# Splitting the state-read matmuls of an f32 attention-and-MLP kernel over two 64-column tiles of the TensorE array

## The chip, the cores and the metric

One core of a Trainium2 chip runs the whole program. The metric is the device time of one execution in microseconds (us); the profiled span is some 2 us shorter than the time of the same run. "Granted clock" is the share of the full TensorE clock that the trace records, 1.0 or 0.5. Kernels of one session are compared with runs of the kernel before on the same chip. "Batch" means one of the eight batch elements of the attention, which the kernel interleaves with the MLP of the batch before it.

## The reference, cut to what matters

```python
B, H, S, Ns, D = 8, 8, 512, 32, 64
scores2 = scale * state @ x^T                      # [B, H, Ns, S]
a2 = exp(scores2 - max); a2 /= a2.sum(-1)          # softmax over the 512 tokens
sread = a2 @ x                                     # [B, H, Ns, D]: the reads of the states
...                                                # xread, the other direction, likewise
h = concat(xread, sread) @ w_in                    # 4352 rows, 512 -> 2048
out = (h * cos(h)) @ w_out                         # 2048 -> 512
```

Everything is f32. The change concerns `sread` alone: for each head a product of 32 x 512 by 512 x 64.

## The kernel before

The eight heads are four pairs (index k) of two (index j). `a2T[:, j, c]` holds the weights of chunk c of 128 tokens, transposed: 128 tokens x (4 pairs x 32 states). One matmul multiplies all 128 columns with the x of all four pairs (256 columns), and of its four by four blocks only the diagonal ones are wanted: pair k's states with pair k's x. `keep` picks them, and `keep2` transposes what it picked for the MLP.

```python
def reads(self, j):
    cols = slice(NK * D * j, NK * D * j + NK * D)      # NK = 4, D = 64: 256 columns
    for c in range(NC):                                # 4 chunks of 128 tokens
        nc.tensor.matmul(
            out=at[:, 0, cols], lhsT=self.a2T[:, j, c, :],
            rhs=self.x_b[:, c].rearrange("p (k j) d -> p j k d", j=2)[:, j],
            start=(c == 0), stop=(c == NC - 1))

def keep(self):
    self.inverse(self.i2)
    src = at[:, 0].rearrange("p (j k d) -> p j k d", j=2, k=NK)
    for k in range(NK):
        rows = slice(Ns * k, Ns * k + Ns)
        nc.vector.tensor_tensor(self.sr[rows], src[rows, :, k, :], ..., op=ALU.mult)
...
LATE = ([("turn", j) for j in range(2)] + [("reads", j) for j in range(2)]
        + [("keep",), ("keep2",)])
```

Around it runs the MLP: `hidden` (two matmuls of 512 columns), the gate on ScalarE and VectorE, `output` (four matmuls of 512 columns). The attention's parts of the next batch are dealt out between them, so one call of `reads` stands before an `output` block and the other before a `hidden` block. `products` and `scores` already use array tiles (64 rows x 32 columns, eight at once). In the first 165 us VectorE and ScalarE also convert the weights, which come as float64.

## Time and profile before

| | before |
|---|---|
| time, median of 3 | 903.25 us (902.56 to 905.52) |
| profiled span | 901.1 us, granted clock 0.973 |
| PE busy | 841.5 us, 93% |
| reads on PE (L311) | 128 instructions, 32.0 us |
| one batch in the saturated part | 94.87 us, PE busy all of it |

From about 170 us on PE works almost without a pause. Before that PE waits for the converted weights and its clock comes and goes, as the page's clock row shows (40 slices of the span, tenths of full speed):

```profile
PEclk9689988999999999999999999999999999999999
```

### The profile page before, as it was taken

Reading aid. Unit: us, or ns where it says so; the run is one execution under the profiler, and the core shown is the slowest. Engines: PE = TensorE matmul, PEld = TensorE weight load, DVE = VectorE, ACT = ScalarE, POOL = GpSimd, SP = SyncE. Lnnn points to the kernel's source line nnn. Section 1 sums busy time; section 2 is a strip of 40 time slices with the busy share of each in tenths; the row PEclk is TensorE's granted clock in tenths of the full one; section 3 lists DMA queues with packets and bytes.
Section 4 is the critical chain, followed back from the end, with each engine's and each line's share of the span. In section 5 each row is a group of like instructions: output and inputs, shape, how many; then the busy total and the mean of one; then the engine's idle time right before and its main releaser. Section 6 shows DMA issues by size and latency. Waiting matters only on the chain.

```text
span 901.1 us, 7084 instructions
## 1 busy us (share of the span) xinstructions
PE 841.5 (93%) x2720; PEld 385.2 (43%) x2720; DVE 356.7 (40%) x520; ACT 408.9 (45%) x631; POOL 0.7 (0%) x6
## 2 busy tenths in 40 slices
PE   3569867899999999999999999999999999999997
PEld 2134324244534453444444443445344534444664
DVE  4687885335322443245224522353225322222121
ACT  2546563355344634464344525453455344434332
POOL 0000000000000000000000000000000000000000
PEclk9689988999999999999999999999999999999999
DMA  6632630021000300030003000300010000000100
GB/s 163 186 141 96 184 140 1 0 70 24 1 1 23 71 0 1 1 93 1 0 1 93 1 0 1 91 4 1 1 47 1 0 1 23 24 0 1 47 1 23
DMA packets 45377, 35.05 MB, mean 39 GB/s; under 512 B 36384, under 2 KB 36384, under 8 KB 45344
## 3 DMA queue, kind: packets, MB, share of 16 engines
q1 hardware_dynamic: 44256, 34.35, 13.4%
q8 instruction: 21, 0.34, 0.2%
q10 hardware_dynamic: 1088, 0.26, 0.2%
q14 instruction: 12, 0.10, 0.0%
HBM read 25.69 MB, written 8.91 MB: 38 GB/s over the span
## 4 chain that ended last, share of the span: by engine, by line
PE 86%; DVE 7%; ACT 4%; issue 1%; DMA 0%; ACTq 0%; DVEq 0%
PE o L403 48%; PE h L373 28%; PE at L245 5%; PE at L311 3%; PE at L219 1%; DVE e L176 1%; ACT e L165 1%; ACT raw L166 1%; DVE w_in L189 1%; PE at L300 1%; DVE w_in L179 1%; ACT q L379 1%; ACT q L388 1%; DVE w_out L189 1%; DVE q L382 1%
## 5 line engine op out<-in xcount | busy, mean ns | idle before, releaser
L403 PE MATMUL o<-w_out,g 128*128 128x512 f32 x1088 | 495.3, 597 | 5.9 <-DVE w_out L189 5.9
L403 PEld LDWEIGHTS o<-w_out,g 128*128 128x128 f32 x1088 | 204.4, 192 | 249.3 <-issue 236.7
L373 PE MATMUL h<-aT,sw 128*128 128x512 f32 x512 | 250.9, 613 | 4.1 <-ACT sw L343 3.4
L382 DVE SCALAR_TENSOR_TENSOR q<-q,h 128x512 f32<-128x512 f32 (+1 forms) x144 | 94.3, 655 | 348.0 <-ACT q L379 348.0
L379 ACT ACTIVATE q<-h 128x512 f32<-128x512 f32 (+1 forms) x144 | 82.5, 573 | 276.1 <-PE h L373 276.1
L393 DVE TENSOR_TENSOR g<-h,q 128x512 f32<-128x512 f32 (+1 forms) x144 | 95.2, 661 | 158.9 <-ACT q L388 158.7
L373 PEld LDWEIGHTS h<-aT,sw 128*128 128x128 f32 x512 | 96.4, 195 | 128.3 <-issue 111.2
L387 ACT ACTIVATE q<-q 128x512 f32<-128x512 f32 (+1 forms) x144 | 87.2, 606 | 105.2 <-DVE q L382 105.2
L388 ACT ACTIVATE q<-q,halfpi 128x512 f32<-128x512 f32 (+1 forms) x144 | 100.5, 698 | 4.5
L245 PE MATMUL at<-w_in,stT 64*32 64x512 f32 (+1 forms) x528 | 41.6, 606 | 24.1 <-DVE w_in L189 12.2
L343 ACT COPY sw<-at 128x1024 f32<-128x1024 f32 (+1 forms) x33 | 32.3, 978 | 43.6 <-PE at L245 43.6
L311 PE MATMUL at<-x_b,a2T 128*128 128x256 f32 x128 | 32.0, 396 | 4.0 <-DVE a2T L303 4.0
L311 PEld LDWEIGHTS at<-x_b,a2T 128*128 128x128 f32 x128 | 25.3, 199 | 13.9 <-issue 6.5
L373 PE MATMUL h<-sT,w_in 128*128 128x256 f32 x128 | 30.2, 379 | 0.0
L245 PEld LDWEIGHTS at<-w_in,stT 64*32 64x32 f32 x528 | 6.8, 106 | 54.8 <-DVE w_in L189 17.8
L373 PEld LDWEIGHTS h<-sT,w_in 128*128 128x128 f32 x128 | 24.3, 190 | 10.1 <-issue 5.0
L409 ACT ACTIVATE ot<-o 128x512 f32<-128x512 f32 x34 | 19.4, 596 | 19.8 <-DMA out_dram<-ot 14.7
L165 ACT ACTIVATE e<-e,ebias 128x1024 int32<-128x1024 int32 (+1 forms) x18 | 18.9, 1051 | 11.4 <-DVE e L162 11.4
L219 PEld LDWEIGHTS at<-ident,x_b 128*128 128x128 f32 x112 | 13.8, 141 | 16.7 <-issue 12.0
L263 DVE STREAM_TRANSPOSE spread<-m 128x1024 f32<-128x1024 f32 x16 | 19.8, 1236 | 0.0
L176 DVE SCALAR_TENSOR_TENSOR e<-raw,e 128x1024 int32<-128x1024 int32 (+1 forms) x18 | 19.7, 1096 | 0.0
L226 ACT COPY xT<-at 128x512 f32<-128x512 f32 x28 | 16.0, 571 | 8.1 <-PE at L219 8.1
(49 smaller groups left out, 269.5 us busy)
## 6 DMA issues: line engine op xcount, KB each, us to landing
x_b<-in_x_dram SPq DMA_DIRECT2D x32, 256.0 KB, 4.7
raw<-in_moe_w_out_dram SPq DMA_DIRECT2D x8, 1024.0 KB, 4.8
out_dram<-ot SPq DMA_DIRECT2D x32, 256.0 KB, 2.2
raw<-in_moe_w_in_dram SPq DMA_DIRECT2D x6, 1024.0 KB, 5.2
raw<-in_moe_w_in_dram SPq DMA_DIRECT2D x4, 512.0 KB, 5.4
out_dram<-ot SPq DMA_DIRECT2D x8, 64.0 KB, 1.7
st<-in_state_dram ACTq DMA_DIRECT2D x4, 64.0 KB, 3.2
st<-in_state_dram SPq DMA_DIRECT2D x4, 64.0 KB, 3.0
```

The source lines that it names most:

```text
L165: nc.scalar.activation(e, e, func=ACTF.Relu, bias=ebias, scale=8.0)
L176: nc.vector.scalar_tensor_tensor(out=e, in0=raw[:, :, :, 1], scalar=-2 ** 31, in1=e, op0=ALU.bitwise_and, op1=ALU.bitwise_or)
L245: nc.tensor.matmul(out=at[Ns * k:Ns * k + Ns, j, 0:n], lhsT=w[D * j:D * j + D, self.b, Ns * k:Ns * k + Ns], rhs=r(slice(D * j, D * j + D), k),
L311: nc.tensor.matmul(out=at[:, 0, cols], lhsT=self.a2T[:, j, c, :], rhs=self.x_b[:, c].rearrange("p (k j) d -> p j k d", j=2)[:, j], start=( ...
L343: nc.scalar.copy(sw_of[self.b, nt][:, :, c0:c1], at[:, :, 0:c1 - c0])
L373: nc.tensor.matmul(out=t.hp, lhsT=t.lhs(i), rhs=t.rhs(i), start=(i == 0), stop=(i == t.kn - 1))
L379: nc.scalar.activation(t.q, t.hp, func=ACTF.Copy, bias=MAGIC)
L382: nc.vector.scalar_tensor_tensor(out=t.q, in0=t.q, scalar=MAGIC, in1=t.hp, op0=ALU.subtract, op1=ALU.subtract)
L387: nc.scalar.activation(t.q, t.q, func=ACTF.Abs)
L388: nc.scalar.activation(t.q, t.q, func=ACTF.Sin, bias=halfpi, scale=-TWO_PI)
L393: nc.vector.tensor_tensor(t.g[:, 0:t.n], t.hp, t.q, op=ALU.mult)
L403: nc.tensor.matmul(out=acc[i], lhsT=t.g[:, P * i:P * i + P], rhs=w_out[:, t.f, :], start=(t.f == 0), stop=(t.f == NF - 1))
```

## The change

Intent: of the sixteen blocks that `reads` computes, twelve are thrown away. Two tiles of 64 array columns take two pairs each, and each streams only the 128 columns of its own pairs, so that eight of the sixteen are no longer computed; both tiles are to run at the same time. A switch between whole-array instructions and tiles is called a mode change below. Its price in the trace has two parts: the drain, a gap of some 93 ns before the next block starts, and the exposed load, the first weight load of that block, which no streaming hides.

```diff
         def reads(self, j):
-            cols = slice(NK * D * j, NK * D * j + NK * D)
+            cols = slice(2 * D * j, 2 * D * j + 2 * D)
             for c in range(NC):
-                nc.tensor.matmul(
-                    out=at[:, 0, cols], lhsT=self.a2T[:, j, c, :],
-                    rhs=self.x_b[:, c].rearrange(...)[:, j],
-                    start=(c == 0), stop=(c == NC - 1))
+                x_c = self.x_b[:, c].rearrange("p (k j) d -> p j k d", j=2)
+                for k in range(0, NK, 2):
+                    rows = slice(Ns * k, Ns * k + 2 * Ns)
+                    nc.tensor.matmul(
+                        out=at[rows, 0, cols], lhsT=self.a2T[:, j, c, rows],
+                        rhs=x_c[:, j, k:k + 2], start=(c == 0),
+                        stop=(c == NC - 1), tile_position=(0, Ns * k))

         def keep(self):
-            src = at[:, 0].rearrange("p (j k d) -> p j k d", j=2, k=NK)
+            src = at[:, 0, 0:4 * D].rearrange("p (j k d) -> p j k d", j=2, k=2)
...
-                    self.sr[rows], src[rows, :, k, :],
+                    self.sr[rows], src[rows, :, k % 2, :],
```

More of the change, by code (lines that the diff above doesn't have):

```diff
@@ L308, in reads @@
         def reads(self, j):
-            cols = slice(NK * D * j, NK * D * j + NK * D)
+            cols = slice(2 * D * j, 2 * D * j + 2 * D)
             for c in range(NC):
-                nc.tensor.matmul(
-                    out=at[:, 0, cols], lhsT=self.a2T[:, j, c, :],
-                    rhs=self.x_b[:, c].rearrange("p (k j) d -> p j k d",
-                                                 j=2)[:, j],
-                    start=(c == 0), stop=(c == NC - 1))
+                x_c = self.x_b[:, c].rearrange("p (k j) d -> p j k d", j=2)
[5 more added lines that the diff above has]
+                        stop=(c == NC - 1), tile_position=(0, Ns * k))
         def keep(self):
             self.inverse(self.i2)
-            src = at[:, 0].rearrange("p (j k d) -> p j k d", j=2, k=NK)
+            src = at[:, 0, 0:4 * D].rearrange("p (j k d) -> p j k d", j=2,
+                                              k=2)
             for k in range(NK):
```

## The prediction

> **What bounds the kernel now.** I read the page first, then the stretch table over single batches, then PE's waits, then PE's timeline inside one batch, then the chain of waits.
>
> The page's busy row and its rows for the changed instruction (engine, operation, operands, count | busy us, mean ns | idle before):
>
> ```profile
> PE 841.5 (93%) x2720; PEld 385.2 (43%) x2720; DVE 356.7 (40%) x520; ACT 408.9 (45%) x631; POOL 0.7 (0%) x6
> ...
> L311 PE MATMUL at<-x_b,a2T 128*128 128x256 f32 x128 | 32.0, 396 | 4.0 <-DVE a2T L303 4.0
> L311 PEld LDWEIGHTS at<-x_b,a2T 128*128 128x128 f32 x128 | 25.3, 199 | 13.9 <-issue 6.5
> ```
>
> To see: 8 batches x 2 head halves x 4 chunks are 64 matmuls of the source, but x128 records: each f32 matmul is two load-and-multiply pairs. All reads together are 32.0 us of PE, so even a reads that cost nothing could save 3.5% at most.
>
> The stretch table (stretch, length, busy time of each engine, granted clock, DMA):
>
> ```profile
> 235.26:330.13 94.87, 94.87 (x314) 42.33 (x313) 33.25 (x49) 44.03 (x68) 0.00 (x0) 1.00 0.09 23
> 330.13:425.00 94.87, 94.87 (x314) 42.33 (x313) 33.25 (x49) 44.03 (x68) 0.00 (x0) 1.00 0.09 23
> ...
> 0.00:160.00 160.00, 109.46 (x351) 49.33 (x352) 114.12 (x149) 79.56 (x107) 0.70 (x6) 0.86 0.43 128
> ```
>
> To see: from about 235 us on PE is busy the whole of every 94.87 us batch at full clock, VectorE for 33 us and ScalarE for 44 us of it. PE's waits after 240 us, asked for alone, are an empty list. A microsecond taken from PE there is a microsecond of the end. Before 160 us it is different: PE 109 of 160 us, VectorE 114 (the weights' conversion), clock 0.86.
>
> PE's timeline in the third batch (start, length, PE, line, operation, count):
>
> ```profile
> 236.99 3.60 PE L403 MATMUL o<-w_out,g 128*128 128x512 f32 x8
> 240.42 1.89 PE L311 MATMUL at<-x_b,a2T 128*128 128x256 f32 x8
> 242.15 1.88 PE L373 MATMUL h<-aT,sw 128*128 128x512 f32 x4
> ...
> 252.75 1.88 PE L373 MATMUL h<-aT,sw 128*128 128x512 f32 x4
> 254.56 1.09 PE L245 MATMUL at<-w_in,stT 64*32 64x512 f32 x16
> 255.58 3.70 PE L403 MATMUL o<-w_out,g 128*128 128x512 f32 x8
> 259.21 1.09 PE L245 MATMUL at<-w_in,stT 64*32 64x512 f32 x16
> ```
>
> To see: one call of reads runs from 240.42 to 242.15: 1.73 us, 216 ns an instruction, pure streaming. L403 takes (240.42-236.99)/8 = 429 ns for twice the columns, so nothing but columns counts. And L245, the products, already run as array tiles (64 rows x 32 columns, eight of them): 16 instructions that would take 16 x 427 ns = 6.8 us one after the other take 1.02 us. This block is my measuring stick.
>
> **What the Trainium skill says.** (1) "TensorE: Matmul & The Clock Gate", Part 3: Packing small matmuls, says that matmuls on different column tiles of the array run at the same time, three of 32 columns measured at 2.38x. The trace agrees for the products: records of single instructions put the eight first starts at 254.558 to 254.605 us, 7 ns apart, and the eight second ones at 255.012 to 255.058. These overlap across column tiles on the same rows too, which the reads need. (2) The same section says that a weight load overlaps a running matmul only when the row group differs. The products disagree: the second load of a tile starts at 254.585 and the second matmul comes 454 ns after the first, which is 427 of streaming plus only the first, exposed load. (3) "TensorEngine Tiling (Array Packing)", Key Properties, says that changing the tiling mode drains TensorE. The trace shows it at both edges: L373 should release the array at 252.75 + 4x0.43 = 254.47, the tile block starts at 254.56, 0.09 us late; and it should end at 255.058 + 0.427 = 255.485, but L403 starts at 255.578, again 93 ns late. (4) "TensorE: Matmul & The Clock Gate", LDWEIGHTS (loading the stationary operand), says a load takes its columns over 1.2 GHz. Agrees: the load that the drain exposes costs 27 ns in front of 32-column tiles (454-427) and about 105 ns in front of 128 columns (the L403 block after the products is 3.70 long instead of 3.60).
>
> **The change part by part.**
> Removed: a call's 8 instructions of 256 columns over the whole array, 8 x 216 = 1.73 us.
> Added: 16 instructions of 128 columns a call, in two chains of eight (upper and lower 64 array columns), with 16 loads of 64 columns. A chain must be serial: its instructions use the same cells. Columns per instruction halve: 427/4 = 107 ns in the tile form (512 columns took 427). If the two chains run beside each other, the stream is 8 x 107 = 0.855 us. The loads, an estimated 64/1.2 = 53 ns each between 27 and 105, fit beside 107 ns of streaming of the same tile.
> Added: two mode changes a call, since every neighbour of a reads call is a full-array matmul: drain in 0.093 + exposed first load 0.053 + second tile's start 0.007 + drain out 0.092 + exposed 128-column load 0.105 = 0.35 us.
> A call then is 0.855 + 0.35 = 1.205 us against 1.728: 0.52 saved, not 0.87.
> Moved: nothing. Instruction order on every engine is as before apart from the doubled reads. The four VectorE products of keep stay 32x128 elements, 287 ns each; their source only lies closer together. It is correct for PSUM: the tiles write different 32-row quadrants, and the second half starts only after the first is complete.
>
> Where it counts. Batches 2 to 7: 12 calls on a saturated PE: 12 x 0.52 = 6.3 us. The chain of waits decides the other two (start, length, what):
>
> ```profile
> 48.91 2.61 PE h L373 x4
> 51.54 0.60 ACT q L379
> ...
> 148.51 3.78 PE at L311 x8
> 152.29 3.83 PE o L403 x8
> 156.12 1.73 PE at L311 x8
> 157.84 1.73 PE h L373 x4
> 159.60 0.61 ACT q L379
> ```
>
> Batch 0: the chain jumps over its reads (51.3 to 54.8 us), and goes on through VectorE's conversions, back to back, on which PE then waits: I count 0. Batch 1: both calls lie on it, and the first runs at half clock, 3.57 us for 8 (427 ns each). At half clock it would be some 2.1 us, so 1.5 us of cold time goes, worth 0.75 us if the clock comes back at the same moment and the work behind it moves into the cold stretch. With the second call's 0.52: 1.25 us. Behind it hidden, gate, VectorE and keep follow in a chain, so it is passed on.
> Sum: 6.3 + 1.25 = 7.5 us. I take 0.6 off for the per-instruction floor (full-array instructions show 216 instead of 213 ns) and for a chain that starts a slot late in some calls: 6.9 us, 903.25 - 6.9 = 896.3 us.
>
> **The rivals.**
> A: the two chains don't overlap. For: they share all 128 rows, and two moving streams of 128 partitions each are shown by no instruction here (products stream 64-row halves). Against: four products tiles stream through the same rows at once. It would make 16 x 107 = 1.71 + 0.35 = 2.06 us, 0.33 more a call: 12 x 0.33 + 0.7 = about 5 us slower, 908.
> B: the loads become the bound. Two 53 ns loads fall on every 107 ns slot; if one port serves both, that is 100% of it, and any extra of 20 ns makes 8 x 20 = 0.16 us a call, 2 us in all: 898.5. Against: eight loads of the products start within 48 ns.
> C: free switches, if the drain is hidden. Then 0.87 a call, 12 to 13 us, 890.5. Against: each of the products blocks from 254 to 260 us pays the same 0.09 and 0.10.
> D: the wait moves. keep2's transpose waits 0.13 us a batch for VectorE's keep, which hangs on the gate of the hidden matmul behind reads. Both come earlier by the same time, so the wait stays and costs nothing new. If it grew by all that reads 1 gives up, 6 x 0.5 = 3 us would go: 899.5.
>
> **Range and chances.** Main line 896.3; B and D lie 2 to 3 us above, C 6 below, A 12 above. I give A one chance in ten, B and D together two. Executions before spread from 902.56 to 905.52, partly because the clock's cold stretches before 170 us fall differently. So 893.5 to 900.5 should hold it 8 times in 10. Faster by over 2% means under 885.2, which even C misses: 1%. Slower by over 2% means over 921.3, beyond A: 1%.
>
> **What would show it.** The reads row should be 256 records of form 128 rows x 64 columns, 128 moving. In the batch stretches PE stays busy throughout and 94.87 becomes about 93.85. Starts of the two chains should lie about 7 ns apart and a chain's steps about 107 ns. The full-array block behind each call should be 0.10 longer, with 0.09 us gaps at both edges. Steps of 107 ns alternating between the chains mean A; steps of 120 to 160 ns in both mean B; no gaps mean C; keep2 idle of over 0.3 us means D. A batch stretch above 94.87 makes the prediction wrong; so does a total gain that comes from before 160 us.

## The result, and the profile after

The changed kernel takes 894.56 us, median of 6 runs (891.99 to 897.16), against 903.08 us of the kernel before (902.40 to 905.52, 6 runs). Ratios in this document are the mean time of one kernel's fast runs over that of the other's of the same rounds, so they are not quite the ratio of the medians. Here the ratio is 0.9899, with a 95% interval of 0.9876 to 0.9922, which is 9.1 us less (7.0 to 11.2). Where a gain "by the ratio" is given below, it is one minus the ratio times the mean of the kernel before in that session, 903.6 to 904.6 us.

The page of the changed kernel, its busy row and the two rows of the reads (the line is now L315):

```profile
PE 833.5 (93%) x2848; PEld 373.8 (42%) x2848; DVE 356.7 (40%) x520; ACT 408.7 (46%) x631; POOL 0.7 (0%) x6
...
L315 PE MATMUL at<-x_b,a2T 128*64 128x128 f32 x256 | 18.2, 288 | 4.0 <-DVE a2T L303 4.0
...
L315 PEld LDWEIGHTS at<-x_b,a2T 128*64 128x64 f32 x256 | 14.4, 142 | 15.1 <-issue 9.9
```

Twice as many records, of half the array (128*64) and half the columns, cover 18.2 us instead of 32.0. VectorE and ScalarE did the same work as before.

The stretch of one saturated batch (stretch, length, busy time of PE, weight loads, VectorE, ScalarE, GpSimd, clock, DMA):

```profile
326.23:420.09 93.86, 93.86 (x330) 40.83 (x329) 33.24 (x49) 44.03 (x68) 0.00 (x0) 1.00 0.10 23
```

PE is still the bound and still never stops; the batch is 1.01 us shorter (94.87 - 93.86). Over five batches the stretches add up to 474.34 us before and 469.31 after, so six are worth 6.04 us. About 3 us of the 9.1 must come from before them: the third batch's reads begin at 232.37 us instead of 235.26.

PE's timeline around the two calls of the third batch:

```profile
230.56 1.88 PE L377 MATMUL h<-aT,sw 128*128 128x512 f32 x4
232.37 1.09 PE L315 MATMUL at<-x_b,a2T 128*64 128x128 f32 x16
233.39 3.70 PE L407 MATMUL o<-w_out,g 128*128 128x512 f32 x8
237.02 1.09 PE L315 MATMUL at<-x_b,a2T 128*64 128x128 f32 x16
238.05 1.98 PE L377 MATMUL h<-aT,sw 128*128 128x512 f32 x4
```

L377 would hand over at 230.56 + 4 x 0.43 = 232.28, and the tiles start at 232.37: the drain. The blocks behind the calls are 3.70 and 1.98 long instead of 3.60 and 1.88: the exposed load. The records of single instructions in the trace give the rest (starts in ns from the first of a call, of a call in the sixth batch, and the next full-array matmul):

```
lower half    0  160  269  379  488  597  706  815
upper half    7  167  276  385  494  604  713  822
next matmul   1024, and the one after it at 1558 instead of 1024 + 429
```

The two chains run 7 ns apart, in steps of 109 ns. A call costs 93 (drain in) + 1024 + 105 (exposed load) = 1222 ns, where it cost 1728.

The chain of waits at batch 1, where the clock is half:

```profile
147.85 1.97 PE at L315 x16
149.82 5.52 PE o L407 x8
155.34 1.02 PE at L315 x16
156.37 1.93 PE h L377 x4
```

The first call fell from 3.78 us to 1.97, but the output block behind it grew from 3.83 to 5.52. By the trace's clock records the half clock covers 146.1 to 153.0 us before and 146.8 to 153.6 after, the same 6.83 us; it caught the work for 4.4 us after the reads' start before, and for 5.7 us after, so the work that moved forward ran in it. Of what the first call saved, 0.12 us were left: from its start to that of the second call it is 3.78 + 3.83 = 7.61 us before and 7.49 after.

### The profile page after: what moved, and what is told of

The parts are those of the page before. It is cut to its first block, busy times and chain, and to the rows that moved or that the text cites. A ratio compares the mean times of both kernels' runs of the same rounds, so it can differ in the third digit from the quotient of the medians.

```text
span 892.1 us, 7340 instructions
## 1 busy us (share of the span) xinstructions
PE 833.5 (93%) x2848; PEld 373.8 (42%) x2848; DVE 356.7 (40%) x520; ACT 408.7 (46%) x631; POOL 0.7 (0%) x6
## 4 chain that ended last, share of the span: by engine, by line
PE 86%; DVE 7%; ACT 4%; issue 1%; DMA 0%; ACTq 0%; DVEq 0%
PE o L407 49%; PE h L377 28%; PE at L245 5%; PE at L315 2%; PE at L219 1%; DVE e L176 1%; ACT e L165 1%; ACT raw L166 1%; DVE w_in L189 1%; PE at L300 1%; DVE w_in L179 1%; ACT q L383 1%; ACT q L392 1%; DVE w_out L189 1%; DVE q L386 1%
## 5 line engine op out<-in xcount | busy, mean ns | idle before, releaser
L377 PE MATMUL h<-aT,sw 128*128 128x512 f32 x512 | 250.3, 612 | 4.1 <-ACT sw L347 3.4
L377 PEld LDWEIGHTS h<-aT,sw 128*128 128x128 f32 x512 | 95.1, 194 | 127.7 <-issue 112.5
L377 PE MATMUL h<-sT,w_in 128*128 128x256 f32 x128 | 30.2, 379 | 0.0
L377 PEld LDWEIGHTS h<-sT,w_in 128*128 128x128 f32 x128 | 24.3, 190 | 10.1 <-issue 5.0
L315 PE MATMUL at<-x_b,a2T 128*64 128x128 f32 x256 | 18.2, 288 | 4.0 <-DVE a2T L303 4.0
L315 PEld LDWEIGHTS at<-x_b,a2T 128*64 128x64 f32 x256 | 14.4, 142 | 15.1 <-issue 9.9
```

The lines of the kernel that those rows point to most:

```text
L315: nc.tensor.matmul(out=at[rows, 0, cols], lhsT=self.a2T[:, j, c, rows], rhs=x_c[:, j, k:k + 2], start=(c == 0), stop=(c == NC - 1), tile_p ...
L377: nc.tensor.matmul(out=t.hp, lhsT=t.lhs(i), rhs=t.rhs(i), start=(i == 0), stop=(i == t.kn - 1))
```

## The experiments

Ten kernels besides the change were run for the questions that the traces leave: is it really overlap, does the order of the program matter, what does the change of tiling cost, how far does the idea go, and where do the 3 us before the saturated part come from. All gave correct results except the first.

### Both products on the same half of the array (same_half)

```diff
+            for k in range(0, NK, 2):
+                for c in range(NC):
-                        out=at[rows, 0, cols], lhsT=self.a2T[:, j, c, rows],
+                        out=at[0:2 * Ns, 0, 256 * (k // 2) + cols...],
+                        lhsT=self.a2T[:, j, c, rows],
-                        stop=(c == NC - 1), tile_position=(0, Ns * k))
+                        stop=(c == NC - 1), tile_position=(0, 0))
...
```

> Both products of a call put on the same 64 array columns (results wrong on purpose: the second pair's sums land in the wrong rows). Same instructions, columns and loads as the change, no second place to run. Theory (the gain is the overlap of two chains on the two halves of the array): 16 steps of 109 ns in a row, a call 0.093 + 0.053 + 16 x 0.109 + 0.095 + 0.105 = 2.09 us against 1.22 in the change and 1.73 before; a steady batch 93.86 + 2 x 0.87 = 95.6 us; median 10 to 12 us above the change, slower than before. Rival (the gain comes from smaller loads or shorter instructions, not from overlap): the batch stays within 0.3 us of 93.86.

Measured: 907.86 us, ratio 1.0054 (1.0028 to 1.0080), slower than before by 4.9 us. The trace has 16 starts of one chain at 0, 160, 269, ... 1688 ns, each 109 after the last, and the next matmul at 1891. A batch of it, by stretch:

```profile
441.70:537.29 95.59, 95.59 (x330) 42.56 (x329) 33.25 (x49) 44.04 (x68) 0.00 (x0) 1.00 0.09 23
```

95.59 us, against 95.6 expected. With the same number of instructions, columns and loads, and the second place gone, the gain turns into a loss. The loop order is turned too; half_by_half below has that order with both places and a batch of 94.83, so in this order the second place alone is worth 0.76 us a batch. The median is 13.3 us above the change, a little over the 10 to 12 expected; 10.4 of it (6 x 1.73) lie in the six batches. It is overlap, and its price without overlap is what rival A of the prediction had said for one call.

### The same tiles, one half after the other in the program (half_by_half)

```diff
-            for c in range(NC):
-                x_c = self.x_b[:, c].rearrange("p (k j) d -> p j k d", j=2)
-                for k in range(0, NK, 2):
+            for k in range(0, NK, 2):
+                for c in range(NC):
+                    x_c = self.x_b[:, c].rearrange("p (k j) d -> p j k d", j=2)
```

> The change with the order of a call turned: four chunks of the lower half, then four chunks of the upper half, instead of alternating. Theory (each tile takes its instructions as soon as its own predecessor is done, whatever the order in the queue): starts still in pairs 7 ns apart, batch 93.86 us. Rival (matmuls start strictly in program order[...]): the second chain starts only beside the last step of the first, 15 steps instead of 8, a call about 1.98 us, a batch about 95.4 us.

Measured: 904.5 us in one look (903.01 before), a batch of 94.83 us. The batch is the evidence here; the third batch's reads begin 1.9 us later than before in this one execution. Both expectations missed. The timeline and the starts of single instructions:

```profile
426.86 1.58 PE L315 MATMUL at<-x_b,a2T 128*64 128x128 f32 x16
428.38 3.70 PE L407 MATMUL o<-w_out,g 128*128 128x512 f32 x8
```

```
lower half    0  160  270  379  488  597  706  815
upper half                      494  654  763  872  982  1090  1200  1309
next matmul   1511
```

The records don't name the half; the two chains are told apart by their steps of 109 ns and by the first step of 160, which has an exposed load in it. The compiled program has the lower half's eight before the upper half's eight. So the ninth starts at 494 ns, ahead of the sixth (597), and starts are not strictly in program order. But it doesn't start at 7 ns either: it comes beside the fifth, when three of the lower half still wait. It looks as if only a few waiting instructions of one tile can be passed; that number is read off this one pattern and not tested further. The result is 12 steps instead of 8, which the two mode changes eat up: 94.83 against 94.87 before. In the saturated batches nearly the whole gain hangs on the loop order, chunk outside and half inside.

### Both calls of a batch in one place (together)

```diff
         def reads(self, j):
+            if j == 1:
+                self.reads_one(0)
+                self.reads_one(1)
+
+        def reads_one(self, j):
```

> The change with both calls of a batch issued one after the other, in the place of the second: one mode change in and out instead of two. Theory (each mode change pair costs 0.093 in, 0.053 and 0.105 of exposed loads, 0.095 out): a batch saves about 0.35 us, 93.51 us, in all 6 x 0.35 = 2.1 us below the change. Rival (the gaps at the edges are not the price of the mode change and turn up elsewhere, or a block of 64 instructions runs the queue dry): a batch of 93.8 us or more.

Measured: 887.13 us, ratio 0.9814 (0.9791 to 0.9837). A batch is 93.51 us, exactly as expected: one mode change pair less saves 0.35 us, so the gaps are its price and turn up nowhere else. The 32 instructions of a block run through in steps of 109 ns up to the last; the queue doesn't run dry.

But the kernel is 7.4 us below the change in the medians, where six batches explain 2.1. The timeline at batch 1 shows the surplus (last column: idle before, and what ended it). Before the change:

```profile
143.84 0.66 PE L300 MATMUL at<-ident,z 128*128 128x128 f32 x4 [1.56 <-DVE a2T L303]
148.51 3.78 PE L311 MATMUL at<-x_b,a2T 128*128 128x256 f32 x8 [4.01 <-DVE a2T L303]
```

With both calls together:

```profile
144.16 3.60 PE L412 MATMUL o<-w_out,g 128*128 128x512 f32 x8
148.35 1.97 PE L320 MATMUL at<-x_b,a2T 128*64 128x128 f32 x32 [0.59 <-DVE a2T L303]
```

The first call waits 4 us for VectorE's copy of a2T, and the output block stood behind it in PE's order. With the call moved behind that block, the block fills the wait, and the reads then run at full clock. That was a side effect of the edit, so it was tried by itself further down (moved_whole).

### Four tiles of 32 columns (four_tiles)

```diff
-            cols = slice(2 * D * j, 2 * D * j + 2 * D)
+            cols = slice(D * j, D * j + D)
-                for k in range(0, NK, 2):
-                    rows = slice(Ns * k, Ns * k + 2 * Ns)
+                for k in range(NK):
+                    rows = slice(Ns * k, Ns * k + Ns)
-                        rhs=x_c[:, j, k:k + 2], start=(c == 0),
+                        rhs=x_c[:, j, k], start=(c == 0),
...                                     # keep reads the first 2 * D columns
```

> One step further: four tiles of 32 columns, one head pair each, 64 columns moving. Theory (streaming of the longest chain plus the mode change): 8 steps of 53 + 2.5 = 56 ns, a call 0.093 + 0.027 + 0.446 + 0.020 + 0.095 + 0.105 = 0.79 us, batch 93.86 - 2 x 0.43 = 93.0 us, median 5 to 6 us below the change. Rival (issue is the bound: 32 load and multiply pairs cannot start every 14 ns, say one in 27): 32 x 27 = 0.87 us, the batch stays at 93.8 to 93.9; 56 to 109 ns a step lies between.

Measured: 889.19 us, ratio 0.9825 (0.9794 to 0.9856), 5.4 us below the change in the medians, in the expected range. The call in the timeline:

```profile
424.30 0.65 PE L315 MATMUL at<-x_b,a2T 128*32 128x64 f32 x32
424.88 1.99 PE L376 MATMUL h<-aT,sw 128*128 128x512 f32 x4
```

The single records show four chains 7 ns apart: 0, 80, 136, 192, ... 415 ns, a first step of 80 (a 27 ns load and 53 of streaming) and then 56 each, and the next matmul at 584. A call is 93 + 584 + 105 = 782 ns, a batch 92.98 us where 93.0 was expected. Issue is no bound here: 32 load and multiply pairs start within 435 ns.

### Tiles in the saturated batches only, and in the early ones only (late_only, early_only)

```diff
+        def reads(self, j):
+            if self.b >= 2:          # early_only: self.b < 2
+                self.reads_tiles(j)  # as changed
+            else:
+                self.reads_whole(j)  # as before
...                                    # keep likewise
```

> Tiles in batches 2 to 7 only, whole-array reads in batches 0 and 1. Theory (the saturated batches pay 6 x 1.01 us, and what the change gained above that, some 3 us by the traces, lies before batch 2): batches of 93.86 us, median 6 us below before, 896.5 to 897.5, 2 to 3 above the change. Rival (the extra 3 us of the change are the luck of when the clock comes back and not tied to the early reads): median within 1 us of the change's 894.5.

> The complement: tiles in batches 0 and 1 only. Theory of the prediction: 0 from batch 0 and 1.25 us from batch 1, median 901.5 to 902.5. Rival (the early reads are worth the 3 us that the one pair of traces shows): 899.5 to 900.5. Batches from 2 on stay at 94.87 us.

Measured: late_only 898.25 us, ratio 0.9933 (0.9910 to 0.9955), 6.1 us by the ratio; its batches are 93.86 us, but for one of 94.58, in which an output block waits 0.45 us for ScalarE. That is 3.7 us above the change, so the rival falls; this distance (2 to 3 expected) and the absolute range were missed, by about the 1.2 us by which before was slower in those rounds (904.25) than in those of the change (903.08). early_only 901.13 us, ratio 0.9964 (0.9939 to 0.9989), 3.3 us (1.0 to 5.5); its batches are 94.87 us. The median lies between the two ranges. The two add up to 9.3 (6.06 + 3.26), against 9.1 for the change. The split is clear: the six saturated batches pay what their length says, and the early reads are worth something more, with an interval that holds both the predicted 1.25 us and the 3 us of the trace. Its size leans on the mix of executions of before: in that session five of eleven took 905.64 to 907.30 us, at a mean granted clock of 0.964 to 0.967, while all six of early_only lie at 0.971 to 0.974. Against the six of before at 0.972 or 0.973 (mean 902.9) early_only gains 2.1 us.

### Whole-array reads, moved in batch 1 only (moved_whole)

```diff
 # against the kernel before
         def reads(self, j):
+            if self.b != 1:
+                self.reads_one(j)
+            elif j == 1:
+                self.reads_one(0)
+                self.reads_one(1)
+
+        def reads_one(self, j):
```

> The kernel before, whole-array reads, with one thing altered: in batch 1 both calls of reads are issued in the place of the second. Theory for the surplus of the run with both calls together (7.4 us where mode changes explain 2.1): the output block that stood behind the wait for VectorE's copy now fills that wait, 4.0 us of idle becomes about 0.6, and the clock is warm when the reads come. Then this kernel gains 4 to 6 us with no tile at all, 897 to 899. Rival (the surplus is clock luck or belongs to tiles): within 1.5 us of before. Batches from 2 on stay at 94.87 us either way.

Measured: 900.23 us against 904.25 before in that session, ratio 0.9955 (0.9929 to 0.9982), 4.1 us (1.6 to 6.4). The timeline shows the wait filled, and both calls at full clock:

```profile
147.19 3.60 PE L410 MATMUL o<-w_out,g 128*128 128x512 f32 x8
151.38 3.72 PE L318 MATMUL at<-x_b,a2T 128*128 128x256 f32 x16 [0.59 <-DVE a2T L303]
```

The size is at the low end of the expected 4 to 6; the absolute figure lies over the range of 897 to 899. Here too the slower executions of before weigh: against its six at the higher clock the gain is 2.5 us, and in the two traces the third batch's reads begin 2.8 us sooner. So a good part of the surplus of the run with both calls together (7.4 - 2.1 = 5.3 us) has nothing to do with tiles, and was to be had in the kernel before; how large a part is not settled.

### Both improvements (four_tiles_together)

The edits of four_tiles and together in one kernel.

> Both improvements: four tiles of 32 columns and both calls in one place. Theory (they add): one block a batch of 16 steps of 56 ns + 0.14 + mode change = 1.23 us where the change spends 2.44, a batch of 92.65 us, 7.3 us in six batches and about 5 in batch 1: 881 to 883. Rival (128 instructions in under 1 us run the queue dry, or they share a gain): batch 92.9 or more, 884 to 887.

Measured: 877.95 us, ratio 0.9720 (0.9693 to 0.9746): the only version that beats the kernel before by over 2%, by 25 us, and it beats the change by 16.6 in the medians. The block and the batch:

```profile
412.38 1.10 PE L320 MATMUL at<-x_b,a2T 128*32 128x64 f32 x64
413.42 1.98 PE L381 MATMUL h<-aT,sw 128*128 128x512 f32 x4
```

```profile
420.52:513.16 92.64, 92.64 (x362) 40.15 (x361) 33.22 (x49) 44.03 (x68) 0.00 (x0) 1.00 0.09 23
```

All 64 instructions and their loads run through in steps of 56 ns, and the batch is 92.64 us, as the sum of the parts says. The time fell below the expected 881 to 883 because the early part gave more: keep2's transpose of batch 1 starts at 154.83 us instead of 163.53 in the change, and in this run the clock stayed at full speed from 127 us to the last block.

### Where the early microseconds come from (batch0_only, batch1_only)

The traces of before and after differ in the clock between 58 and 71 us. The same three stretches, before (the figure before the last two is the granted clock):

```profile
58.00:62.00 4.00, 3.17 (x8) 1.14 (x6) 3.86 (x8) 3.45 (x4) 0.00 (x0) 1.00 0.37 152
62.00:66.00 4.00, 2.01 (x16) 0.35 (x16) 3.89 (x8) 0.00 (x0) 0.00 (x0) 0.78 0.73 264
66.00:71.00 5.00, 3.87 (x12) 1.33 (x5) 0.33 (x1) 1.01 (x1) 0.00 (x0) 0.50 0.00 0
```

and after:

```profile
58.00:62.00 4.00, 4.00 (x6) 1.61 (x6) 3.97 (x7) 3.46 (x4) 0.00 (x0) 0.57 0.43 176
62.00:66.00 4.00, 2.90 (x19) 0.50 (x17) 3.79 (x9) 0.00 (x0) 0.00 (x0) 1.00 0.68 253
66.00:71.00 5.00, 3.87 (x13) 1.69 (x10) 1.43 (x4) 2.46 (x3) 0.00 (x0) 1.00 0.02 9
```

Before, the half clock fell on the products and hidden matmuls at 65 to 71 us, which lie on the chain. After, it fell on the output block at 58 us, under which VectorE is busy for 3.97 of 4 us and sets the pace. keep2 of batch 0 came 2.0 us sooner (69.35 instead of 71.36 us). In the ten kernels profiled up to here, keep2 of batch 0 started at 68.6 to 69.6 us in the five with two or four tiles at once in batch 0, and at 71.4 to 71.8 in the five others (before, late_only, moved_whole, same_half, half_by_half). It looked like a cause. Tiles in one early batch alone (`self.b == 0` or `self.b == 1` in the edit above) tested it:

> Tiles in batch 0 alone. Theory (the shorter reads of batch 0 leave PE idle for 2.2 instead of 0.8 us before the output block, so that the half-clock window falls on that block, where PE waits for VectorE anyway, and no longer on the products and the hidden matmuls at 65 to 71 us): keep2's transpose of batch 0 starts at 69.0 to 69.8 us instead of 71.4 to 71.8, granted clock 0.5 to 0.7 at 58 to 62 us and 1.0 at 64 to 70; the median is about 2 us below before. Rival (that shift is chance, or is lost again by the later windows): keep2 at 71 us or later, or the median within 0.7 us of before.

> Tiles in batch 1 alone. Theory of the prediction: 1.25 us below before, and batch 0 with its half-clock window at 65 to 71 us as before. Rival (in batch 1 the clock's windows decide, and the shorter reads are worth between nothing and 3 us by chance): executions spread by 3 us or more, median anywhere within 2 us of before.

Measured: batch0_only 902.58 us, ratio 0.9982 (0.9963 to 1.0000), 1.6 us by the ratio (0.0 to 3.3); the medians differ by 0.46 us, as its rival said. batch1_only 900.96 us, ratio 0.9967 (0.9947 to 0.9988), 3.0 us (1.1 to 4.8); the interval just holds the theory's 1.25 us, and its executions spread over 2.8 us with a median 2.1 below before, just outside both figures of its rival. The theory for batch 0 falls as a mechanism. In batch0_only keep2 did come early (69.93 us), but without the half-clock window on the output block:

```profile
58.00:60.00 2.00, 1.62 (x4) 0.87 (x5) 1.97 (x4) 1.00 (x1) 0.00 (x0) 1.00 0.98 371
68.00:70.00 2.00, 1.89 (x5) 0.89 (x6) 0.00 (x0) 0.06 (x1) 0.00 (x0) 1.00 0.00 0
```

And batch1_only, whose batch 0 reads are those of before, has keep2 at 69.33 us and clock 1.00 in both stretches too. The neat pattern was chance, or has a cause that these traces don't show. What does hold in all of them is the form: the clock's records change between 1.0 and 0.5 in pieces of 3.41 us and multiples of it, between 17 and some 170 us and again only at the very end, and which work falls under a half-clock piece differs from kernel to kernel and from run to run. The executions of before in that session lie between 902.36 and 906.89; that this is why is likely, as the two over 906 are those with the lowest mean clock (0.966 against 0.969 to 0.973), but only one execution of before has a trace.

The traces can bound this luck. Change and early_only have the same code up to the third batch's reads, which begin at 232.37 and 230.16 us; before and late_only do too, and there they begin at 235.26 and 236.81. So the same early code differs by 2.2 and 1.5 us, and the two traces with early tiles are on average 4.8 us ahead of the two without.

In the pair of before and after the lead can be followed. It is 2.0 us after batch 0, falls by 1.4 where only the change has a half-clock piece (133 to 136 us), grows by 0.6 over the reads of batch 1 to 1.3 at keep2 of batch 1, and by 1.7 where only before has one (167 to 170 us). The hidden blocks that these two pieces hit, in the chain of waits before:

```profile
134.70 2.00 PE h L373 x4
166.62 3.61 PE h L373 x4
```

and after:

```profile
132.65 3.38 PE h L377 x4
165.32 1.91 PE h L377 x4
```

So in this pair the batch 1 reads themselves account for some 0.6 of the 2.9 us, and the rest lies in what the half-clock pieces hit. Whether the shorter reads steer those pieces or not, and how the early 3 us split between batch 0, batch 1 and luck over many executions, stays open.

## Why the prediction was right or wrong

The time, 894.56, lies in the range of 893.5 to 900.5, below the middle of 896.3. Point by point:

**What bounds the kernel** was right. PE stays busy through every batch after 232 us, and late_only gives 6.1 us for 6.04 us of shorter batches: passed on one for one.

**The stream and the mode change** were right, nearly to the nanosecond. Foretold were 0.855 + 0.35 = 1.205 us a call; measured are 1.222. Of the 17 ns, 15 are a floor of 2.5 ns an instruction: the six steps after the first are 109 instead of 107. For this and for late starts the prediction took 0.6 us off as a whole. A batch of "about 93.85" is 93.86. The drain is 93 in and 95 out, the exposed load 53 in and 105 out, and together shows that a pair of them costs 0.35 us. The tile products, which were in the kernel already, were a good measuring stick for what the new tiles would do.

**Rival A** (no overlap) is dead: the starts lie 7 ns apart, and same_half shows what A would have cost. It was closer than the prediction thought, though. The prediction argued from tiles and not from order, and half_by_half shows that the same tiles in the other loop order give next to nothing, 0.04 us a batch. It got the benefit of the change's order without seeing that it was needed: that was luck.

**Rival B** (loads) is dead: 109 ns steps, and in four_tiles 56 ns, with loads of all tiles between them. **Rival C** (free switches) is dead: the gaps are there. **Rival D** (keep2's wait): L377 of the changed kernel at 243.30 + 4 x 0.43 ends at 245.02 and keep2 starts at 245.15, so the wait is 0.13 us, as before.

**The step that was probably mis-sized is "Where it counts"**, for the first two batches: "I count 0" for batch 0 and "1.25 us" for batch 1. Measured by early_only they are worth 3.3 us, with 1.0 to 5.5 in the interval, so 1.25 is not excluded but is at its low end. The 0.75 us of the first call assumed that "the clock comes back at the same moment". It didn't, counted from the work: in the profiled pair the half clock ended 4.4 us after the first call's start before and 5.7 us after the change, and left 0.12 us of the 0.75. (A reading was a little off as well: the call's 3.57 us are a first step of 588 ns and seven of 427, not eight of 427.) Elsewhere the half-clock pieces moved: those at 64 to 71 us and 167 to 170 us were absent after the change, and others at 58 to 61 and 133 to 136 us were new. The chain of waits could not show that. It tells which work was waited for in one execution, and not at what clock the same work will run in the next kernel. The prediction's range allowed for it; its point value did not. So what the saturated batches gave was foretold, and how far the time fell below the middle of the range was in part the clock's luck.

The prediction also named, as a sign of being wrong, a total gain that comes from before 160 us. About a third of it does, by early_only, so that sign came out in part; in the profiled pair 1.3 us of lead stood at keep2 of batch 1, at 164 us, and the other 1.7 came just after it.

## What to carry to other kernels

Array tiles pay for a product with unwanted blocks when its tiles are issued in turn, one instruction for each, and when the streaming saved is well above the price of a mode change pair, 0.35 us here; so put neighbouring tile work in one block, and try smaller tiles where the data allows: here those of 32 columns, which compute nothing unwanted, beat those of 64. Take the cost of a new tile form from a tile block that the trace already has, drains and exposed loads included. And where a block stands behind a wait on another engine, look first at whether other work can stand before it: that was worth 4.1 us here (1.6 to 6.4), against 3.3 (1.0 to 5.5) for the early tiles, with no tile at all.

## What the Trainium skill lacked or had wrong

- "TensorE: Matmul & The Clock Gate", Part 3: Packing small matmuls, says that matmuls start and end in program order. In half_by_half the ninth instruction started at 494 ns and the sixth at 597. Nor does that section spell out that the order of issue decides on the overlap: alternating tiles took 8 steps of 109 ns, one tile after the other 12.
- The same section says, under what overlaps and what doesn't, that a weight load overlaps a running matmul only on other row groups, while its paragraph on the mechanism also lets a load go ahead into a background weight buffer. The runs side with the second: both tiles use all 128 rows, the loads are recorded as 137 ns in the median, and the steps are 109 ns, 2.5 more than the streaming of 107.
- "TensorEngine Tiling (Array Packing)", Key Properties, names the drain at a change of tiling mode without a size. It was 93 ns in and 95 ns out, with first loads of 53 and 105 ns exposed on top, 0.35 us for a pair.
